# Another machine model orders the queues of a recurrence and expert-layer kernel on one core

## The chip, the cores and the metric

The kernel runs on one core of a Trainium2 chip. The metric is the device time of one execution in microseconds (us). TensorE (PE) multiplies, with its weight loads shown as PEld; VectorE (DVE), ScalarE (ACT) and GpSimd (POOL) work on elements; SyncE (SP) issues most of the DMAs. Each engine works through its own queue of instructions in order, and semaphores make an instruction wait for others.

## The reference

A gated linear recurrence over 768 tokens, for 4 sequences and 8 heads of width 48, and then a SiLU layer of width 2048 over all 3,072 tokens:

```
for t in range(S):
    state = alpha[:, :, t, :, None] * state + einsum('bhd,bhe->bhde', k[:, :, t], v[:, :, t])
    y[:, :, t] = einsum('bhd,bhde->bhe', q[:, :, t], state)
x = y.transpose(0, 2, 1, 3).reshape(B * S, H * D)
h = x @ w_in
out = (h * (1 / (1 + exp(-h)))) @ w_out
```

## The kernel before

The program has a quick path, `quotients` (L356), and a slow one, `general`, which is taken when a check of the inputs' sizes fails; with these inputs it is not taken. All below is `quotients`. The check's flag is loaded by each engine shortly before the end, with a hint for the branch.

**The work.** The 3,072 tokens are 24 chunks of 128, in six groups of four. A chunk goes through attention stages on several engines, and each group then through w_in, SiLU and w_out. From the second half of the second group on, products by w_in are made as 20 products of sums of blocks (`enter`, L943), and products by w_out as seven (`leave`, L1050).

The weights arrive as 64-bit floats and are converted on ScalarE (L637) and VectorE (L653 to L655) in the first stage.

**Attention, from the ninth chunk on.** `load` (L466) issues eight DMAs each for alpha, k and q of a chunk (L485) into the tiles at, kt and qt, of which there is one each. `beside` (L491) makes two ScalarE copies in each (L496). `turned` (L715) transposes a tile on VectorE (L716): at into al, kt and qt into the tile turn, of which there is one; behind it, `load` for the next chunk may begin. `products` scans (L742) and forms kp (L759, L761); `quotient` forms p by reciprocals (L772), a scan (L774) and a product (L780). `flip` (L782) transposes kp on VectorE into turn (L790) and stores it to the DRAM tile flips by a DMA of SyncE (L792); `land` (L794) brings it back as kn on GpSimd's queue. `scores` multiplies kp and p on TensorE, copies the result out of PSUM on ScalarE (L828, L831) and masks it on GpSimd; `values` multiplies with v and copies to xt (L873); `states` adds to the state on VectorE (L890).

**The layer.** `enter` has three PSUM banks (ps_m). A product goes into a bank, and ScalarE copies it out (L963) to g or part, or VectorE combines it there (L971). SiLU is L968. `side_by_side` adds halves (L1046), `leave` has two banks (ps_o) and subtracts parts of g (L1062); results are stored at L1074.

**The check of the inputs.** `audit` (L665) loads alpha and the weights anew and reduces them on VectorE (L706). Its last sixteen loads, those of w_out, land in at, kt and qt.

**What sets the order.** The code emits work in steps: `fill` deals out pieces of the layer between the attention stages of each step. The language then makes each engine's queue when the program is built: it runs the instructions through a model of the machine and issues what that model has ready, by priority. An instruction inside `tc.keep_in_program_order` stays behind what was emitted ahead of it on its engine. After `settle` (L1197), which opens the tiles of the later stages, all TensorE's instructions are held so (L381 to L392), and some of VectorE's: the sums of weights and tokens and the reductions of the check.

Of the kernel before, what the change touches and what calls it, by code (L numbers as in the profile page):

```python
# [1291 lines left out]
@with_exitstack  # L1292
def kernel(
    ctx: ExitStack,
    tc: tile.TileContext,
    q: bass.AP,
    k: bass.AP,
    v: bass.AP,
    alpha: bass.AP,
    moe_w_in: bass.AP,  # L1300
    moe_w_out: bass.AP,
    out: bass.AP,
):


    flag = ctx.enter_context(tc.tile_pool(name="flag", bufs=1))
    small = flag.tile([1, 1], I32, name="small")
    args = (q, k, v, alpha, moe_w_in, moe_w_out, out)
    within = quotients(tc, small, *args)
    with tc.If(within < 1, label="general"):  # L1310
        general(tc, *args)

# [29 lines left out]
```

## Time and profile before

| | |
|---|---|
| median of 3 runs | 557.59 us (557.36 to 560.03) |
| the profiled execution | 558.21 us |
| its span, first to last instruction | 556.5 us |
| granted clock of TensorE | 0.999 of full speed |
| TensorE busy | 539.6 us |
| VectorE busy | 440.8 us |
| ScalarE busy | 253.8 us |
| GpSimd busy | 106.8 us |
| mean DMA rate | 109 GB/s |

The span leaves out what comes ahead of the first and behind the last instruction. A line of the page's groups names line, engine, operation, what is written and read and its shape, the count, the busy time and the mean of one, and then the idle time of the engine just ahead of it with what ended it. A line of the waits names who waited for whom, the total in us, the times and the longest. A line of a time line has the start, the length, the engine (SPq is SyncE's sequencer, which issues DMAs), the operation and the count. A window's line has its ends, its length, and for PE, PEld, DVE, ACT and POOL the busy time and the instructions, and then TensorE's clock, the share of the DMA engines and GB/s. A line of DMA issues ends with the KB of each and the median us from issue to landing.

### The profile page before, as it was taken

The numbers are of one execution on the slowest core, as the hardware profiler recorded it, in microseconds if no ns is written. First come the engines' busy times: TensorE is split into PE (matmuls) and PEld (weight loads), VectorE is DVE, ScalarE is ACT, GpSimd is POOL, SyncE is SP. The second block draws the span as 40 slices with busy tenths as digits, with TensorE's granted clock in tenths as the row PEclk, the third lists the DMA queues.
The fourth block names the chain that finished last, engine by engine and source line by source line (L and its number), as shares of the span: only waits on it lengthen the run. The fifth ranks groups of instructions, "written<-read, shape, count | busy, mean of one in ns | idle before, by whom it ended". The sixth has DMA issues, their size and how long they took to land. (4 is left out here: it accounts for less than half of the span.)

```text
span 556.5 us, 13238 instructions
## 1 busy us (share of the span) xinstructions
PE 539.6 (97%) x5010; PEld 487.0 (88%) x5010; DVE 440.8 (79%) x826; ACT 253.8 (46%) x570; POOL 106.8 (19%) x194
## 2 busy tenths in 40 slices
PE   6999999999999899999999999999999999999995
PEld 4788887998898699899999898999998999999995
DVE  5897888987997899997997988897863896945431
ACT  2556653235564564573555465555453341423100
POOL 3110000222334213223214213212111000001000
PEclk9999999999999999999999999999999999999999
DMA  9988971134434434435646564446331135500000
GB/s 213 255 230 220 235 191 29 38 71 87 86 69 107 93 68 95 99 72 145 141 79 159 129 149 104 104 96 150 106 115 46 53 109 172 156 7 23 15 23 25
DMA packets 121496, 60.72 MB, mean 109 GB/s; under 512 B 108497, under 2 KB 110161, under 8 KB 121425
## 3 DMA queue, kind: packets, MB, share of 16 engines
q1 hardware_dynamic: 117968, 52.73, 40.7%
q0 software_dynamic: 3456, 7.08, 4.1%
q8 instruction: 40, 0.66, 0.5%
q14 instruction: 32, 0.25, 0.2%
HBM read 51.90 MB, written 7.86 MB: 107 GB/s over the span
## 5 line engine op out<-in xcount | busy, mean ns | idle before, releaser
L388 PE MATMUL ps_o<-w_out,g 128*128 128x192 f32 x768 | 134.0, 328 | 0.5 <-DVE o L1071 0.5
L388 PEld LDWEIGHTS ps_o<-w_out,g 128*128 128x128 f32 x768 | 125.6, 190 | 3.6 <-DVE o L1071 0.8
L388 PE MATMUL ps_o<-wt,g 128*128 128x192 f32 x576 | 99.8, 327 | 0.0
L388 PE MATMUL ps_m<-xt,w_in 128*128 128x256 f32 x396 | 94.8, 383 | 1.8 <-ACT xt L873 1.1
L388 PEld LDWEIGHTS ps_o<-wt,g 128*128 128x128 f32 x576 | 95.1, 190 | 1.6 <-issue 0.2
L388 PEld LDWEIGHTS ps_m<-xt,w_in 128*128 128x128 f32 x396 | 73.4, 190 | 13.3 <-ACT xt L873 1.6
L388 PE MATMUL ps_m<-xc,w_in 128*128 128x256 f32 x324 | 79.6, 382 | 1.1 <-DVE g L971 1.1
L388 PEld LDWEIGHTS ps_m<-xc,w_in 128*128 128x128 f32 x324 | 60.4, 190 | 9.1 <-DVE g L971 1.5
L1074 POOL DMA_DIRECT2D out_dram<-o x40 | 22.4, 559 | 202.6 <-DVE o L1071 102.6
L1062 DVE TENSOR_TENSOR g<-g 128x512 f32<-128x512 f32 x72 | 49.2, 698 | 9.1 <-PE ps_o L388 8.9
L388 PE MATMUL ps_m<-xc,wx 128*128 128x256 f32 x216 | 56.4, 383 | 0.0
L968 ACT ACTIVATE g<-g 128x1024 f32<-128x1024 f32 x36 | 37.1, 1055 | 40.8 <-DVE g L971 40.7
L963 ACT COPY g<-ps_m 128x512 f32<-128x512 f32 x72 | 40.8, 588 | 29.3 <-PE ps_m L388 28.8
L835 POOL TENSOR_SCALAR_AFFINE_SELECT g<-g 64x256 f32<-64x256 f32 x64 | 38.2, 596 | 60.2 <-ACT g L828 57.1
L971 DVE TENSOR_TENSOR g<-ps_m,g 128x512 f32<-128x512 f32 x63 | 41.9, 684 | 5.1 <-PE ps_m L388 4.2
L388 PEld LDWEIGHTS ps_m<-xc,wx 128*128 128x128 f32 x216 | 39.5, 190 | 4.7 <-ACT kt L496 0.2
L742 DVE TENSOR_TENSOR_SCAN u<-al,one 128x516 f32<-128x516 f32 x24 | 29.9, 1246 | 11.9 <-ACT al L739 11.7
L963 ACT COPY part<-ps_m 128x512 f32<-128x512 f32 x36 | 21.2, 589 | 37.5 <-DVE g L971 22.2
L800 POOL DMA_DIRECT2D kn<-flips x48 | 26.2, 553 | 49.2 <-PE ps_a L388 43.2
L774 DVE TENSOR_TENSOR_SCAN p<-al,inv 128x516 f32<-128x516 f32 x24 | 29.8, 1241 | 2.6 <-PE ps_a L388 2.1
L706 DVE TENSOR_REDUCE seen<-bits 128x1 f32<-128x512 int32 (+1 forms) x33 | 26.6, 825 | 5.7 <-DMA bits<-in_alpha_dram 2.9
L823 POOL TENSOR_SCALAR_AFFINE_SELECT g<-g 128x512 f32<-128x512 f32 x16 | 12.6, 808 | 85.8 <-ACT g L822 85.8
(133 smaller groups left out, 694.4 us busy)
## 6 DMA issues: line engine op xcount, KB each, us to landing
bits<-in_moe_w_in_dram SPq DMA_DIRECT2D x24, 512.0 KB, 4.3
bits<-in_moe_w_out_dram SPq DMA_DIRECT2D x16, 384.0 KB, 3.7
bits<-in_alpha_dram SPq DMA_DIRECT2D x9, 512.0 KB, 4.0
out_dram<-o POOLq DMA_DIRECT2D x40, 96.0 KB, 2.3
at<-in_alpha_dram SPq DMA_DIRECT2D x128, 24.0 KB, 2.3
kt<-in_k_dram SPq DMA_DIRECT2D x128, 24.0 KB, 2.1
qt<-in_q_dram SPq DMA_DIRECT2D x128, 24.0 KB, 2.0
flips<-turn SPq DMA_DIRECT2D x12, 256.0 KB, 4.3
```

Of the source, the lines that this page charges most:

```text
L388: in_order(nc.tensor.matmul(*args, **kw))
L706: dve.tensor_reduce(seen[kind][which][:, i : i + 1], x, axis=AX, op=op, apply_absolute_value=True))
L742: dve.tensor_tensor_scan(u[:, end - 1 :: -1], sg[:, end:0:-1], one[:, end:0:-1], 0.0, ALU.mult, ALU.add)
L774: dve.tensor_tensor_scan(p[:, 0:end], sg[:, 0:end], iv[:, 0:end], 0.0, ALU.mult, ALU.add)
L800: gps.dma_start(c["kn"][32 * i : 32 * i + 32], x[i])
L823: gps.affine_select(g[:, u], g[:, u], pattern=[[0, NP], [1, C]], compare_op=ALU.is_ge, fill=0.0, base=0, channel_multiplier=-1)
L835: gps.affine_select(x, x, pattern=[[0, NP], [1, CH]], compare_op=ALU.is_ge, fill=0.0, base=0, channel_multiplier=-1)
L963: act.copy(to, ps)
L968: act.activation(x, x, AF.Silu)
L971: dve.tensor_tensor(to, a, b, op)
L1062: dve.tensor_tensor(cells(grp, h, pair, *to), cells(grp, h, pair, *x), cells(grp, h, pair, *y), ALU.subtract)
L1074: (gps if grp < NG - 1 else nc.sync).dma_start(out[r : r + C, c * HO : (c + 1) * HO], o)
```

## The change

`quotients` is emitted inside a block whose queues are ordered by the language's other model of the machine. The instructions, tiles and pools stay as they are, the orders that the code pins too. The block is one of its own in the program, with a branch behind it to the place of the test of the flag.

```diff
     args = (q, k, v, alpha, moe_w_in, moe_w_out, out)
-    within = quotients(tc, small, *args)
+    with tc.block(name="quick", schedule_with_timeline_sim=True):
+        within = quotients(tc, small, *args)
     with tc.If(within < 1, label="general"):
         general(tc, *args)
```

## The prediction

> **What bounds the kernel now.** The first view is the page's busy times, the second the table of windows, the third TensorE's own waits.
>
> ```profile
> span 556.5 us, 13238 instructions
> PE 539.6 (97%) x5010; PEld 487.0 (88%) x5010; DVE 440.8 (79%) x826; ACT 253.8 (46%) x570; POOL 106.8 (19%) x194
> ```
>
> ```profile
> 109.00:200.00 91.00, 87.42 (x992) 78.28 (x991) 78.07 (x156) 48.88 (x126) 30.77 (x50) 1.00 0.42 83
> 200.00:250.00 50.00, 49.87 (x475) 45.63 (x474) 49.34 (x97) 28.52 (x67) 11.62 (x21) 1.00 0.40 82
> 250.00:300.00 50.00, 50.00 (x579) 45.59 (x578) 44.33 (x79) 25.32 (x61) 12.88 (x24) 1.00 0.55 131
> ```
>
> ```profile
> PE ps_a L388 <- DVE p L780: 1.6, 2, 0.9
> PE ps_m L388 <- DVE g L971: 1.4, 2, 1.1
> PE ps_m L388 <- ACT part L963: 0.6, 1, 0.6
> PE ps_o L388 <- DVE o L1071: 0.5, 1, 0.5
> PE ps_m L388 <- ACT xt L873: 0.3, 1, 0.3
> ```
>
> TensorE is the bound: from 109 us to the end it stands idle 4.4 us (the sum of the last view, taken over that window), at a granted clock of 1.00 (the column behind POOL). So an order can win little there. What it can lose shows in the second row: between 200 and 250 us VectorE is busy 49.34 of 50 us. A wait put into its queue there has no idle time to go into.
>
> The other views are those of the loop that brings in alpha, k and q: the page's DMA issues, and the time lines of SyncE, ScalarE and VectorE around 240 us.
>
> ```profile
> at<-in_alpha_dram SPq DMA_DIRECT2D x128, 24.0 KB, 2.3
> flips<-turn SPq DMA_DIRECT2D x12, 256.0 KB, 4.3
> ```
>
> ```profile
> 239.93 3.63 SPq L485 DMA_DIRECT2D kt<-in_k_dram  x8
> 243.66 3.71 SPq L485 DMA_DIRECT2D qt<-in_q_dram  x8
> ```
>
> ```profile
> 238.86 1.07 ACT L963 COPY g<-ps_m 128x512 f32<-128x512 f32 x2
> 239.82 0.60 ACT L963 COPY part<-ps_m 128x512 f32<-128x512 f32 x1
> 240.71 0.94 ACT L496 COPY at<-at 32x256 f32<-32x256 f32 x2 [0.28 <-DMA at<-in_alpha_dram]
> ```
>
> ```profile
> 235.42 0.72 DVE L890 TENSOR_TENSOR st<-ps_a,st 48x192 f32<-48x192 f32 x2
> ```
>
> **The change part by part.** It keeps every instruction (2,569 matmuls, 637 DMAs in both programs) and moves them in the queues: 335 of TensorE's matmuls, 445 of VectorE's 826 instructions, 354 of ScalarE's 569, 263 of SyncE's 551 issues.
>
> *TensorE.* All its moves lie ahead of 109 us; behind that its order is the same, matmul for matmul. Ahead of it, transposes and small matmuls stand between other products than before, and the number of changes from one kind to the next goes from 262 to 265. I cost this at 0. From 24 us on TensorE is hardly idle in that stretch (48.92 of 50 us busy between 50 and 100), so a gain has some 3 us to go into; a few more waits on the conversions of the weights would cost as much. Bounds: -3 and +3.
>
> *The end.* Each engine gets one more branch. VectorE's compare-and-branch starts at 550.80 and its next record stands at 551.40: 0.6 us. The last store, issued at 551.16, lands at 553.75 and covers it. Cost 0; without that cover 0.6.
>
> *The loop of the loads.* One buffer each holds alpha, k and q of a chunk (at, kt, qt). VectorE transposes it (L716), which frees it; SyncE then issues eight loads; ScalarE makes two copies (L496) behind their landing. The rows give the length of a loop from the end of the transpose: seven issues at 0.475 us (3.71 over eight, with the gap) are 3.3, the eighth lands 2.3 later, 5.6 in all, and the two copies take 0.8: 6.4 us. ScalarE works in order, so a copy that stands too early holds up the copies out of PSUM behind it (L963, 0.59 each), which free the banks for which TensorE's next product waits.
>
> I took both orders and put TensorE's times of the profile beside them. For each of these pairs of copies that carries a wait on VectorE, the room is a difference: TensorE's time for which the first instruction behind the copy in ScalarE's queue waits, less TensorE's time for which the last instruction up to the transpose waits in VectorE's queue, less VectorE's work from there through the transpose. Between 200 and 430 us, in the order before, the rooms are 8.8, 11.1, 9.8, 18.5, 12.7, 5.6 and 9.7: one below 6.4. In the order after they are for at 6.2, 4.4, 6.2, 4.4, 6.2, 4.4, 6.5, 7.6; for qt 5.3, 5.9, 5.1, 4.8, 4.4; for kt 5.4, 10.7, 10.9, 6.9, 10.2, 4.3. Thirteen of nineteen are short, by 16.2 us in all, and that with a VectorE that is never late.
>
> It is late. Take the chunk of 232 to 253 us. Its states matmuls (ps_a<-vn,kn) end on TensorE at 232.49 (231.97 plus 0.52); the additions that wait for them alone start at 235.42 in the row above: a lag of 2.9. After the change VectorE has there the two additions and at once the next transpose of at (1.1 of work): done at 232.5 + 2.9 + 1.1 = 236.5, landed at 242.1. ScalarE's queue is: a copy of PSUM, one copy of at, a second of PSUM, the other of at, the third of PSUM. So the second ends at 242.1 + 0.4 + 0.6 = 243.1 where TensorE starts on that bank at 242.21, and the third at 244.1 where it wants 243.07. Before, they ended at 239.93 and 240.42. That is 1.0 us late. A shorter room of the neighbouring chunks works alike; I take 1.0 for each of the ten chunks of 21 us between 211 and 430 us: **10**. From below it is 0: with no lag, a room of 4.4 is 2.0 short, and the bank has 2.3 to spare (239.93 to 242.21). From above all of ScalarE's lateness reaches TensorE: 6.4 + 2.9 - 4.4 = 4.9 a chunk, 49.
>
> *The wait that VectorE gets.* The tile turn has one buffer. The transpose of kp into it (L790) is stored by the DMA to flips, and the next transpose of kt writes it again, so it must wait until that DMA has landed, 4.3 us after its issue. VectorE's work between the two is, for the seven such chunks from 212 us on, 9.3, 7.8, 6.0, 9.8, 3.9, 7.2 and 5.2 us before, and 3.2, 3.6, 1.9, 2.7, 1.9, 2.9 and 3.9 after. Short of 4.3 by 1.1, 0.7, 2.4, 1.6, 2.4, 1.4 and 0.4: **10.0**. Behind that transpose stand the combinations of the products (L971) and the halves' sums (L1062); TensorE waits for both. SyncE's pending loads ahead of the store would add to it; VectorE's 5.7 idle us of the third row of windows would take from it. I take it whole; bounds 0 and 20 (3.7 more, eight loads ahead of the store, in about half of them).
>
> *Between 109 and 200 us.* Chunks are 14 to 19 us here, SyncE issues almost without a break, and the rooms are 7.7 and more. One place is worse: the pair of at that ran at 174.90 now stands between copies that ran at 165.27 and 165.75. Its loads were issued from 168.21; SyncE's one idle gap of the forty us before is 2.5 us, so the earliest landing is 168.2 - 2.5 + 5.6 = 171.3, and the bank behind it is wanted at 167.20. That is 4.1, and I take **4**; bounds 0 and 8 (a second such place).
>
> *The sum.* The profiled execution took 558.21 us for its span of 556.5; the median of the runs is 557.59, 0.6 less. 558.2 + 0 + 10 + 10 + 4 = **582**.
>
> [...]
>
> **The rivals.**
> - *The loop in full* (0.11): every lateness of ScalarE reaches TensorE, 4.9 in each of ten chunks, and 4: 558.2 + 49 + 4 = 611. For it: TensorE without slack, and both delays in one ring. Against it: a late TensorE gives VectorE its lag back.
> - *Absorbed* (0.07): VectorE, which waits less for TensorE in the new order, loses its lag of 2.9; the 2.0 that are missing fit into the bank's 2.3: 558. Against it: 49.34 of 50.
> - *Faster* (0.08): the attention steps that stand earlier take away TensorE's waits on p, g and part. All of them gone is 4.4: 553.8. It decides in the loop: if the loads land within 4.4 us of the transpose, copies included, no room is short. Against it: one issue alone is 0.475, and eight are needed.
> - *No change*, because the order does not change: excluded for VectorE and ScalarE by the moves above, true for TensorE from 109 us on.
>
> **How the numbers follow.** The forecast has 0.74, so the likeliest time is 582. Its low end: 4 for the early place with nothing else passed on, 562. Its high end: twice each of the two tens, and 8, is 606. That holds 0.74 at most, so the range goes on to the loop in full: 562 to 612. Outside are the rivals at 0.08 and 0.07, both below. Half a per cent, 2.8 us, is what a measurement of this kernel can tell from none: faster 0.08, same 0.07, slower 0.74 + 0.11 = 0.85.
>
> **What would show it.** ScalarE's waits on the DMAs of at, kt and qt (34 us over the whole run before: 15.8, 9.3, 9.1) should more than double; VectorE should wait for flips at the transpose of kt, which it does not before; TensorE's waits on L963 and L971 should go from 2 us to some 20, spread over 160 to 430 us, with the stretch behind 430 us as long as before. If ScalarE waits for the loads but TensorE's waits stay small, the absorption is right. If ScalarE does not wait more, the loop of 6.4 is wrong.

## The result, and the profile after

The changed kernel takes 596.38 us (median of 4 runs, 594.82 to 597.96), the kernel before beside it 557.48: a ratio of 1.0688, 95% interval 1.064 to 1.0736. The profiled execution took 597.96 us. Its page begins:

```profile
span 596.1 us, 13255 instructions
PE 554.6 (93%) x5010; PEld 496.2 (83%) x5010; DVE 439.0 (74%) x826; ACT 253.8 (43%) x570; POOL 105.2 (18%) x194
```

The span is 39.6 us longer. VectorE and ScalarE have the same work as before, and TensorE has 15.0 us more busy time for the same matmuls, for which the prediction has no term. The table of windows shows where TensorE stands (first figure behind the length: its busy time; behind POOL: its granted clock):

```profile
109.00:160.00 51.00, 47.47 (x516) 42.71 (x516) 39.48 (x84) 21.15 (x59) 13.02 (x23) 0.97 0.35 69
160.00:215.00 55.00, 46.70 (x539) 39.99 (x538) 44.43 (x84) 29.37 (x74) 14.54 (x28) 0.97 0.43 88
270.00:325.00 55.00, 50.38 (x539) 45.02 (x538) 42.40 (x77) 23.89 (x56) 13.33 (x24) 0.97 0.43 102
440.00:596.00 156.00, 149.91 (x998) 141.08 (x990) 92.45 (x176) 44.76 (x87) 9.93 (x20) 1.00 0.22 67
```

The last 156 us are as before (150.17 busy then, 149.91 now). The loss lies ahead of them, and part of it is clock: 0.97 in three of the rows, where before all had 1.00.

A matmul can be followed from one trace to the other, since TensorE's order is the same from 109 us on. The delay of its start, after less before, is by before's clock 3.4 us at 109 us, 3.7 at 126, 8.4 at 139, 12.3 at 170, 17.8 at 200, 20.9 at 274, 29.7 at 320, 37.6 at 369, 39.7 at 394 and 39.7 at 550: about 3 in the start, 14 between 109 and 200, 22 between 200 and 394, nothing behind. Two lists of waits say on whom (total us, times, longest). TensorE's:

```profile
PE ps_a L388 <- ACT xt L873: 7.1, 4, 2.8
PE ps_m L388 <- DVE xc L594: 6.1, 3, 3.6
PE ps_m L388 <- ACT xt L873: 4.4, 2, 3.5
...
PE ps_m L388 <- ACT g L963: 3.2, 3, 1.5
PE ps_m L388 <- DVE g L971: 3.1, 4, 1.2
PE ps_o L388 <- ACT g L968: 2.7, 2, 2.2
PE ps_m L388 <- ACT part L963: 2.5, 3, 1.1
```

and ScalarE's for the loads (two lines of the list):

```profile
ACT kt L496 <- DMA kt<-in_k_dram: 47.9, 16, 6.1
...
ACT qt L496 <- DMA qt<-in_q_dram: 22.2, 13, 3.8
```

With 15.3 and 9.2 for at, ScalarE stands 94.6 us before those copies; it was 34.2. Behind 109 us TensorE waits 19.0 us for ScalarE (0.9 before) and, with 0.5 for o, 9.7 for VectorE (3.5 before). (Of the 4.4 us of the third line, one wait of 0.9 lies ahead of 109 us.)

One wait read through all queues, the longest on xt (time lines of ScalarE, SyncE and TensorE):

```profile
125.76 0.83 ACT L496 COPY kt<-kt 32x256 f32<-32x256 f32 x2 [3.82 <-DMA kt<-in_k_dram]
129.32 0.89 ACT L496 COPY qt<-qt 32x256 f32<-32x256 f32 x2 [2.73 <-DMA qt<-in_q_dram]
133.10 0.40 ACT L496 COPY at<-at 32x256 f32<-32x256 f32 x1 [2.89 <-DMA at<-in_alpha_dram]
133.53 0.48 ACT L873 COPY xt<-ps_a 128x384 f32<-128x384 f32 x1
```

```profile
119.76 4.67 SPq L485 DMA_DIRECT2D kt<-in_k_dram  x7
124.52 3.73 SPq L485 DMA_DIRECT2D qt<-in_q_dram  x8
128.36 3.70 SPq L485 DMA_DIRECT2D at<-in_alpha_dram  x8
```

```profile
134.06 4.33 PE L388 MATMUL ps_m<-xt,w_in 128*128 128x256 f32 x12 [3.53 <-ACT xt L873]
```

ScalarE's queue has the copies of kt, qt and at one behind the other, and the copy to xt behind them. SyncE issues one tile behind the other, 3.7 us each and 5.3 for kt (the first of its eight loads lies ahead of this view), so each copy waits its turn, and TensorE stands 3.53 us for a copy of 0.48. The tile at had been free since 120.95 (its transpose ran from 120.24 for 0.71); its loads were issued from 128.36, behind those of kt and qt.

Windows of the same place:

```profile
132.00:134.00 2.00, 0.00 (x0) 0.00 (x0) 1.97 (x6) 0.88 (x2) 0.70 (x3) 0.92 0.45 102
134.00:136.00 2.00, 1.94 (x5) 1.58 (x6) 1.96 (x6) 0.41 (x2) 0.00 (x0) 0.50 0.30 48
136.00:138.00 2.00, 2.00 (x8) 1.70 (x7) 2.00 (x5) 0.00 (x0) 0.00 (x0) 0.73 0.19 34
138.00:140.00 2.00, 2.00 (x38) 1.52 (x37) 1.97 (x6) 1.59 (x4) 0.00 (x0) 1.00 0.36 53
```

When TensorE goes on, its clock is at half for some 3.4 us. Such a phase lies at the end of four of the waits (those ending at 134, 170, 298 and 405 us, the last phase 6.8 us long). Over windows of 1 us, busy share times the missing clock comes to 7.5 us.

The account of the 39.7 us of delay: the start 3.4 and, behind it, more waits for ScalarE 18.1, more waits for VectorE 6.2, half speed 7.5. That is 35.2. The other 4.5 are busy time of TensorE: behind 109 us it is busy 12.1 us longer (449.3 for 437.2), of which half speed explains 7.5; the rest stays open.

### The profile page after: what moved, and what is told of

The parts are those of the page before. It is cut to its first block, busy times and chain, and to the rows that moved or that the text cites. A ratio compares the mean times of both kernels' runs of the same rounds, so it can differ in the third digit from the quotient of the medians.

```text
span 596.1 us, 13255 instructions
## 1 busy us (share of the span) xinstructions
PE 554.6 (93%) x5010; PEld 496.2 (83%) x5010; DVE 439.0 (74%) x826; ACT 253.8 (43%) x570; POOL 105.2 (18%) x194
## 5 line engine op out<-in xcount | busy, mean ns | idle before, releaser
L388 PE MATMUL ps_o<-w_out,g 128*128 128x192 f32 x768 | 136.3, 331 | 3.2 <-ACT g L968 2.7
L388 PEld LDWEIGHTS ps_o<-w_out,g 128*128 128x128 f32 x768 | 127.6, 192 | 6.8 <-ACT g L968 3.1
L388 PE MATMUL ps_m<-xc,w_in 128*128 128x256 f32 x324 | 83.0, 393 | 7.4 <-ACT g L963 3.2
L388 PEld LDWEIGHTS ps_m<-xt,w_in 128*128 128x128 f32 x396 | 74.8, 193 | 16.8 <-ACT xt L873 4.7
L388 PE MATMUL ps_m<-xc,wx 128*128 128x256 f32 x216 | 58.6, 395 | 6.1 <-DVE xc L594 6.1
L963 ACT COPY g<-ps_m 128x512 f32<-128x512 f32 x72 | 41.8, 588 | 28.8 <-PE ps_m L388 27.9
L968 ACT ACTIVATE g<-g 128x1024 f32<-128x1024 f32 x36 | 37.1, 1054 | 36.7 <-DVE g L971 36.4
L971 DVE TENSOR_TENSOR g<-ps_m,g 128x512 f32<-128x512 f32 x63 | 42.3, 682 | 4.6 <-PE ps_m L388 4.0
L388 PEld LDWEIGHTS ps_a<-p,kp 48*64 48x64 f32 (+1 forms) x640 | 24.9, 151 | 16.4 <-ACT xt L873 8.0
L388 PE MATMUL ps_a<-p,kp 48*64 48x64 f32 (+2 forms) x640 | 30.5, 264 | 8.2 <-ACT xt L873 7.1
L496 ACT COPY kt<-kt 32x256 f32<-32x256 f32 x32 | 12.9, 402 | 48.5 <-DMA kt<-in_k_dram 47.9
L800 POOL DMA_DIRECT2D kn<-flips x48 | 26.2, 553 | 39.6 <-PE ps_a L388 34.9
L774 DVE TENSOR_TENSOR_SCAN p<-al,inv 128x516 f32<-128x516 f32 x24 | 29.7, 1236 | 4.2 <-PE ps_a L388 3.8
```

Of the source, the lines that this page charges most:

```text
L388: in_order(nc.tensor.matmul(*args, **kw))
L496: act.copy(ctxs[n][name][64 * u + 32 : 64 * u + 64, :, :, 0 : D - 32], ctxs[n][name][r, :, :, 32:D])
L774: dve.tensor_tensor_scan(p[:, 0:end], sg[:, 0:end], iv[:, 0:end], 0.0, ALU.mult, ALU.add)
L800: gps.dma_start(c["kn"][32 * i : 32 * i + 32], x[i])
L963: act.copy(to, ps)
L968: act.activation(x, x, AF.Silu)
```

## The experiments

Theories at the outset. **L**: ScalarE's copies stand too soon behind the loads, and the copies out of PSUM wait behind them. **V**: VectorE's new order holds TensorE up (sums, flips, turns). **S**: SyncE issues the loads in a bad order. After the first runs **A**: loads and VectorE's sums of x, each a trouble of its own; and **C**: a long wait costs clock as well.

Most kernels hold a queue in a given order. They are the changed kernel with the list of one engine's instructions, by number, and edges that only order the issue; what is not listed is ordered by the other model anew, so a free queue is not quite that of the changed kernel.

```diff
+    at = {i.name: i for i in nc.cur_bb.bb.instructions}
+    for queue in QUEUES:
+        for x, y in zip(queue, queue[1:]):
+            tc.add_manual_dep(at[f"I-{y}"], f"I-{x}", mybir.DependencyInfo(
+                mybir.DependencyClass.NoSync, mybir.DependencyReason.DATA), reason="queue")
     return within
```

Lines of these kernels' profiles are shifted by their lists; the text gives the line of the code above.

### The block without the other model

```diff
-    with tc.block(name="quick", schedule_with_timeline_sim=True):
+    with tc.block(name="quick"):
```

> The block stays, the other machine model goes: the queues of PE, DVE, ACT and SP are those of before, instruction for instruction, with one more branch on each engine. All theories: the time of before, 557.5, within 1.7 us. If the block itself (its branches) cost anything, the time would be above 560 and part of the 39 us would have nothing to do with the order.

Measured: 559.47 us, ratio 1.0012 (0.9989 to 1.0035). The block and its branches cost nothing that can be measured; the order is the cause.

### One engine's queue as before

> The changed kernel, but ScalarE's 569 instructions are held in the order that they had before; PE, DVE and SP are ordered by the other model around them. Counted as in the prediction, no room behind the loads of at, kt and qt is then short of 6.4 us (smallest 10.2, against 13 short rooms after the change). VectorE's work between the turn of kp and the next turn into the same tile is short of 4.3 us by some 5 us in all. Theory L (ScalarE's copies stand too soon behind the loads, and the copies out of PSUM wait behind them): only the flips and the start are left, 557.5 + 5 + 4 = 566. Theory V (VectorE's new order holds TensorE up: sums, flips, turns): little comes back, 585 to 595. Theory S (SyncE issues the loads in a bad order): 580 to 595, since SP's order is nearer to after than to before.

> The changed kernel, but VectorE's 826 instructions are held in the order that they had before; PE, ACT and SP are ordered by the other model. Rooms short of 6.4 us: 4 of 15 between 109 and 200 us, 10 of 18 behind, 15.0 us in all (after: 16.2). No wait for flips beyond before's. Theory L: most of the loss stays, 557.5 + 39 less the flips (7) = 589, 582 to 594. Theory V: at most 566. Theory S: 580 to 595.

> The changed kernel, but SyncE's 551 issues are held in the order that they had before; PE, DVE and ACT are ordered by the other model. Rooms short of 6.4 us: 6 of 11 between 200 and 430 us, by 7.3 us in all (after: 13 by 16.2). Theory L: somewhat under half of what is lost behind 200 us stays, and the places around 130 to 190 us stay as ACT has them: 572 to 584. Theory V: 588 to 597. Theory S: at most 566.

Measured: ScalarE's queue as before 584.12 (1.0449, 1.0419 to 1.048); VectorE's 585.12 (1.0464, 1.043 to 1.0499); SyncE's 593.51 (1.064, 1.0594 to 1.0685). Of the 38.9 us that the change costs, 13.7, 12.7 and 4.3 came back (each against the 558.95 of the kernel before, run beside them). None of the three theories holds alone: L had 566 for the first, V and S at most 566 for the second and the third.

With ScalarE's queue as before, its waits for at, kt and qt are down to 14.8 us, and yet the delay is 26 us. TensorE's waits there (L641 is L594, L1018 is L971):

```profile
PE ps_m L435 <- DVE xc L641: 6.6, 3, 3.1
...
PE ps_m L435 <- DVE g L1018: 3.7, 2, 3.1
```

They are VectorE's: the sums of x and the combinations. (The line left out, 4.2 us for the first load, stands before the change too, with 4.3.) With VectorE's queue as before, ScalarE's list is (L559 is L496):

```profile
ACT kt L559 <- DMA kt<-in_k_dram: 50.2, 18, 5.9
ACT at L559 <- DMA at<-in_alpha_dram: 33.0, 16, 4.3
```

With qt that is 102.7 us, more than in the changed kernel. So each queue has a trouble of its own.

VectorE's is read best in the changed kernel's time line (lines between left out):

```profile
394.74 0.42 DVE L590 TENSOR_TENSOR xc<-xt 128x256 f32<-128x256 f32 x1
...
396.28 0.41 DVE L590 TENSOR_TENSOR xc<-xt,xc 128x256 f32<-128x256 f32 x1
...
397.43 1.26 DVE L706 TENSOR_REDUCE seen<-bits 128x1 f32<-128x512 int32 x2
...
400.58 1.18 DVE L742 TENSOR_TENSOR_SCAN u<-al,one 128x516 f32<-128x516 f32 x1
...
402.88 1.28 DVE L706 TENSOR_REDUCE seen<-bits 128x1 f32<-128x512 int32 x2
404.07 0.42 DVE L594 TENSOR_TENSOR xc<-xc,xt 128x256 f32<-128x256 f32 x1
```

Each group has eleven sums of x (L590 to L595), and the products wait for them one after another. Here the reductions of the check and a scan stand among them: from the first of these lines to the L594 on which TensorE waited 3.61 us it is 9.3 us, and was 5.2 before. From the third sum to the last, starts compared, groups two to four take 12.8, 9.7 and 12.8 us, and took 6.0, 6.9 and 6.5.

### Both queues as before

> The changed kernel with the orders of before on both ScalarE and VectorE; PE (ahead of 109 us) and SP are ordered by the other model. With one of the two put back 26 us stayed with ScalarE's, 28 with VectorE's: neither alone is the carrier. Theory A (each of the two queues has a trouble of its own: ScalarE's copies too soon behind the loads, VectorE's sums of x and turns too late; with both put back both are gone): 557.5 and the start's 3 to 4, 561, 558 to 566. Theory S (the order of SyncE's issues holds up whichever queue there is): 572 or more, since SP's order is the other model's in all three.

Measured: 568.7 us, ratio 1.0196 (1.0148 to 1.0243). 26.9 us came back, nearly the sum of 13.7 and 12.7, as theory A has it; but 12 are left where it had at most 8.5, so the two queues are not all. The delay is 3.9 at 109 us and 6.9 at 126 (a wait of 2.43 for VectorE, which has stood 2.39 at the turn of at), and 3.3 more come near 316 us: TensorE waits 1.88 us for L971 and runs at half speed behind it, and VectorE stood 2.72 us before that for a load of the check, which SyncE had issued among those of at. Behind 109 us every engine but SyncE works here in the order of before, so these are the order of SyncE's issues: a third, small part.

### Only the start, only the rest

> All five queues hold the order of before for the instructions traced ahead of the first load of at; behind them the other model orders VectorE, ScalarE and SP. The delay of the changed kernel against before stood at 3.6 us at 115 us and at 39.7 at the end. Theory A, if the start's 3.6 simply add: 596.4 - 3.6 = 593, 588 to 597. If the lateness of the start is what upsets the rest (every later wait follows from it): 575 or less.

> The reverse: the instructions traced ahead of the first load of at are ordered as in the changed kernel, those behind as before. If the start's 3.6 simply add: 557.5 + 3.6 = 561, 559 to 564. If the start is worth nothing by itself: 557.5 within 1.7. If its lateness upsets the rest: over 570.

Measured: 596.14 us (1.0711, 1.0683 to 1.074) with the old start and the new rest; 562.42 (1.0093, 1.0057 to 1.013) with the new start and the old rest. By itself the new start costs 5.7 us, of which 4.1 stand at 109 us in the profile. Taken away from the changed kernel it gives nothing back. That the rest has enough waits into which 4 us disappear is the likely reason, but not shown: the other model ordered that rest anew, and up to 226 us ScalarE and VectorE have some instructions in other places than in the changed kernel. Either way the parts are no simple sum.

### Half of the loads

```diff
-            for g in range(NP):
+            for g in range(NP // 2):
                 for u in range(2):
                     nc.sync.dma_start(c[name][64 * u : 64 * u + 32, g],
```

with all five queues held as in the changed kernel.

> The changed kernel with the same order on all engines, but of the eight loads of each alpha, k and q tile from the ninth chunk on only four are issued (it leaves out the loads of four of the eight heads there; their places keep the filling). The loop gets shorter by four issues of 0.475: 6.4 to 4.5 us, and SP's queue is relieved by 192 issues, 91 us of its time. Rooms short of it: five of 4.3 to 4.4, by 0.7 us in all, instead of thirteen by 16.2. Theory A: what goes by the loads returns, the sums of x and the flips stay: 570 to 582. Theory V (the order of VectorE alone, ScalarE's waits being covered): 590 to 597.

Measured: 570.29 us, ratio 1.0235 (1.0217 to 1.0252). 25 of the 39 us are gone with no instruction of TensorE, VectorE or ScalarE in another place. A load lands no sooner than with all of them (median for kt 1.84 us behind its issue, 1.89 in the changed kernel), so what is saved is issues, and the time for which other DMAs stand behind them in SyncE's queue. ScalarE's waits for the loads fell to 17.0 us. What is left of TensorE's waits behind 100 us (L930 is L594; 7.7 us, three waits):

```profile
PE ps_m L724 <- DVE xc L930: 7.7, 3, 3.1
```

### The sums of x moved

VectorE's list is that of the changed kernel with 24 instructions moved; the other four queues are held too.

> The changed kernel with the same order on all engines, except that on VectorE the last nine of the eleven sums of x (L590 to L595, into xc) of the second, third and fourth group stand with one other instruction between two of them, as they did before, instead of up to six. By the durations of before, the work from the third sum to the last falls from 12.5, 9.6 and 12.7 us to 7.3, 7.2 and 7.3 (before: 5.9, 6.7, 6.3). Theory A (the sums are VectorE's own trouble): TensorE's 6.1 us of waits on the sums (L594) go and with them the half speed behind the wait of 3.61 (3.4 us); some of it is taken up by ScalarE's waits for the loads, which stay: 587, 583 to 593. If the sums are late only because the loads are: 594 to 598.

> Both: half of the loads of alpha, k and q from the ninth chunk on (the other half is left out), and the sums moved; the rest as in the changed kernel. With half of the loads 570.3 us, and TensorE's only long waits behind 100 us are three on the sums, 2.1, 2.5 and 3.1 us, each with 3.3 us at half speed behind it (1.7 lost). Theory A, that loads, sums and start are all of it: 570.3 - 7.7 - 5.0 = 557.6, and not under 557.5 + 3.6 - 1 for the start, so 558 to 563. If a third cause of some size is hidden under the two: over 565.

Measured: sums alone 598.05 us (1.0734, 1.0709 to 1.0759), nothing back where theory A had 583 to 593; with half of the loads 564.92 (1.0112, 1.0071 to 1.0153), 5.4 less than half of the loads alone (6.0 when each is set against the kernel before run beside it) and above the 558 to 563 expected. In the first, the waits on L594 are gone from the list, and the one of 3.61 us with them; ScalarE's copies out of PSUM hold TensorE instead:

```profile
PE ps_m L738 <- ACT part L1313: 7.9, 5, 3.0
PE ps_m L738 <- ACT xt L1223: 4.7, 2, 3.8
```

(L1313 is L963; it was 2.5 for part.) With half of the loads TensorE waited even longer for the sums than in the changed kernel (7.7 us for 6.1), so they are not late because of the loads: they are a trouble of their own, but one that runs beside the loads, and it shows only when those are short. In the second, one wait of 3.02 us on L963 is left, with 6.8 us at half speed behind it, some 6 in all; ScalarE stood 5.04 us for qt before it.

### The copies in program order

```diff
-                act.copy(ctxs[n][name][64 * u + 32 : 64 * u + 64, :, :, 0 : D - 32],
-                         ctxs[n][name][r, :, :, 32:D])
+                tc.keep_in_program_order(
+                    act.copy(ctxs[n][name][64 * u + 32 : 64 * u + 64, :, :, 0 : D - 32],
+                             ctxs[n][name][r, :, :, 32:D]))
```

> The changed kernel with one wish more to the scheduler: the copies of at, kt and qt (L496) stay in program order on ScalarE; everything else is ordered by the other model. No room is then short of 6.4 us in either stretch; VectorE's work from the third sum of x to the last is 6.9, 10.7, 8.3 and 7.8 us in the first four groups (before: 7.5, 5.9, 6.7, 6.3; changed: 8.7, 12.5, 9.6, 12.7). Theory A: the start's 3.6, one late group of sums (about 3 us with its half speed) and small change: 566, 561 to 574. If the loss comes back at other instructions as it did with ScalarE's whole queue put back: 575 to 588.

Measured: 572.89 us, ratio 1.0291 (1.0261 to 1.0321): with this wish 23 of the 39 us are gone. Not the copies alone have moved: the other model orders the rest anew, and 323 of ScalarE's 570 places and 413 of VectorE's 826 hold another instruction than in the changed kernel. The delay is 4.2 at 139 us, 6.7 at 180, 14.3 at 200 and 14.0 at the end. The 7 us of one place are a wait on VectorE, which waits for the tile turn (SyncE, VectorE and TensorE; L793 is L792, L717 is L716):

```profile
177.85 3.74 SPq L485 DMA_DIRECT2D kt<-in_k_dram  x7
181.69 3.70 SPq L485 DMA_DIRECT2D qt<-in_q_dram  x8
185.48 0.38 SPq L793 DMA_DIRECT2D flips<-turn  x1
```

```profile
187.87 0.71 DVE L717 STREAM_TRANSPOSE turn<-kt 128x512 f32<-128x512 f32 x1 [6.19 <-DMA vn<-in_v_dram]
```

```profile
193.50 2.08 PE L388 MATMUL ps_m<-xt,wx 128*128 128x256 f32 x4 [5.25 <-DVE g L972]
```

The transpose of kp had ended at 179.74, but its store to flips stood in SyncE's queue until 185.48, behind eleven of these loads that were still to be issued. (The page names vn, the DMA whose end came nearest; vn is no input of that transpose. The copies of kt had ended at 183.84.) This is the wait for flips of the prediction, and here it reaches TensorE nearly whole.

### A wait of known length, put into the kernel before

```diff
         add(b, True)
+        for _ in range(HOLD.pop(0)):
+            act.copy(scratch, scratch)
         copy(b, s[2])
```

with HOLD = 5, 6, 8, 9, 11, 13, 15, 17, 20, scratch a tile of 128x128, and all queues of the kernel before held.

> The kernel before, its order held on all engines, with 5, 6, 8, 9, 11, 13, 15, 17 and 20 small copies (128x128, some 0.27 us each) on ScalarE ahead of one copy out of PSUM in each of nine products of four blocks. TensorE must wait for that bank: by 1.3 to 5.4 us less the bank's slack of about 1, some 19 us in all. Theory C (a wait of more than about 2 us makes the clock fall to half for 3.3 or 6.7 us behind it, 1.7 or 3.4 lost): the delay at the end is larger than the sum of the waits by 8 to 17, 557 + 19 + 12 = 588. If a wait costs itself alone: the delay is the sum of the waits, about 576, and matmuls behind each wait keep their 0.216 us.

Measured: 570.32 us, ratio 1.0227 (1.0202 to 1.0252): 12.95 us. A small copy took 0.298 us, and the waits were shorter than I had reckoned, 9.5 us in six, the bank having more slack:

```profile
PE ps_m L746 <- ACT g L1324: 9.5, 6, 2.4
```

Two of them, of 2.41 and 2.43 us, have half speed behind them; those of 1.10, 1.44 and 1.76 have none. Windows around the one of 1.76 (first two rows) and the one of 2.41:

```profile
370.00:372.00 2.00, 0.24 (x2) 0.16 (x2) 0.64 (x1) 1.89 (x6) 0.00 (x0) 1.00 0.57 186
372.00:374.00 2.00, 2.00 (x11) 1.79 (x11) 1.69 (x3) 1.38 (x4) 0.00 (x0) 1.00 0.29 51
...
414.00:416.00 2.00, 0.00 (x0) 0.00 (x0) 0.00 (x0) 1.87 (x7) 0.00 (x0) 1.00 0.00 0
416.00:418.00 2.00, 1.88 (x5) 1.59 (x6) 1.41 (x3) 1.41 (x5) 0.00 (x0) 0.62 0.00 0
418.00:420.00 2.00, 2.00 (x7) 1.64 (x7) 1.08 (x2) 0.88 (x2) 0.00 (x0) 0.52 0.48 121
420.00:422.00 2.00, 2.00 (x14) 2.00 (x13) 1.39 (x2) 0.20 (x1) 0.00 (x0) 1.00 0.39 150
```

The delay steps from 2.92 to 5.60 over the wait of 2.41, and on to 7.39 while the clock is low: 1.8 more. At 2.43 it is 9.00, 11.69 and 13.39: 1.7 more. 9.5 + 1.8 + 1.7 is 13.0, close to the 12.95 measured. So a wait can cost clock as well, as theory C has it; that a wait costs itself alone is refuted. Two parts of C failed: the clock cost 3.5 us and not 8 to 17, and a limit of about 2 us is not what decides, since in the kernel with both queues as before a wait of 1.88 us has half speed behind it and one of 2.43 has none.

## Why the prediction was right, and where its sizes were wrong

The sign, the kind and the range were right: slower, through ScalarE's and VectorE's waits in the loop of the loads, 596 in 562 to 612. The forecast of 582 was 14 us short. Step by step:

- *The end, 0.* Right: the delay is the same 39.7 us at 394 and 550 us, and the block alone costs nothing.
- *TensorE's order ahead of 109 us, 0 (-3 to +3).* 3.4 us at 109 us in the profile, 5.7 by itself in time: beyond the bound. That stretch has nearly as much idle time as before (7.1 us, 6.6 then); 3.0 us of the loss are busy time. It is not the order of ScalarE or VectorE, since with both as before 3.9 are still there at 109 us. It is mostly clock. The profile's clock records begin with full speed at 19.04 us before and at 24.44 after (its clock column shows 1.00 ahead of them, too, and the granted clocks of 0.999 and 0.984 over the span leave that time out); ahead of them the same transposes take half as long again. TensorE's groups from 19.5 to 24 us, before and after (count, busy time, mean ns):

```profile
L392 PE MATMUL ps_a<-ident,kp 128*128 128x128 f32 x4 | 0.7, 286 | 0.0
```

```profile
L392 PE MATMUL ps_a<-ident,kp 128*128 128x128 f32 x4 | 1.1, 431 | 0.0
```

They follow one another every 0.11 and 0.21 us. TensorE is busy throughout these 5.4 us; at half speed that is 2.7 of the 3.4 us. With the start of before, full speed came at 17 to 20 us in every kernel here; with the new start at 24 to 27 in seven of ten, but at 10.0 and 11.3 in the two with half of the loads, where 2.4 and 2.9 us of delay are there all the same, and at 7.6 with ScalarE's queue as before, which fell back to half from 14.4 to 24.7. Why the new order keeps TensorE at half speed longer stays open.
- *The loop of the loads, 10, and between 109 and 200 us, 4.* The mechanism was right: half the loads, or their copies in another place, give back 25 and 23 us (both help SyncE's other DMAs too, so some of it is the flips'). The size was wrong by nearly half, and mostly ahead of 200 us: the delay grew there by 14.4 where I had 4, bound 8. My rooms there were 7.7 us and more against a loop of 6.4. But 6.4 is the loop of one tile with SyncE free. Its landing of 2.3 us was not too short: the loads landed a median of 2.3, 2.1 and 2.0 us behind their issue (at, kt, qt) before and 1.9 after. Where the copies of three tiles stand together, SyncE issues 24 loads in one go, and the tile at waited from 120.95 to 128.36 for its turn. I had written that SyncE issues almost without a break there, and took no time for it. Behind 200 us the delay grew by 21.9, near the 10 + 10 of the forecast; that confirms neither term, since the sums, which had no term, are in it and the flips hardly.
- *The wait for flips, 10.* VectorE's own wait came near in the sum, and not chunk by chunk: ahead of the turn of kt in the seven chunks from 212 us on it stood 11.8 us (0, 1.2, 4.3, 2.6, 0, 2.8, 0.8), where kt had landed long before. Two stores landed in 2.0 and 2.9 us and held up nothing; the other five stood in SyncE's queue for 1.0 to 3.0 us first, for which the prediction had taken nothing in its 10. The prediction's reading that VectorE does not wait for flips before the change is wrong. There, too, it stood 4.1, 2.1, 0.8 and 1.9 us at the turn of kt until the store to flips had landed (at 139.63, 170.13, 294.57 and 333.88 us); the profile puts these down to another DMA that ended close by:

```profile
140.00 0.71 DVE L716 STREAM_TRANSPOSE turn<-kt 128x512 f32<-128x512 f32 x1 [4.06 <-DMA at<-in_alpha_dram]
...
334.00 0.71 DVE L716 STREAM_TRANSPOSE turn<-kt 128x512 f32<-128x512 f32 x1 [1.91 <-DMA at<-in_alpha_dram]
```

So the wait grew, over the whole run from 8.8 us to 24.1, and was not new. What failed is "I take it whole": TensorE waited directly behind the seven only 0.74 and 0.95 us. The same wait with SyncE's loads ahead of the store, for which I had 3.7 as an upper bound, reached TensorE with 5.25 us in the kernel with the pinned copies.
- *Not priced: the sums of x.* I named the combinations and the halves' sums as what stands behind VectorE's transpose, and did not look at where the eleven sums went. They are 6.1 us of TensorE's waits; the runs give 5.4 for them once the loads are short and nothing before, so they are no term to be added but a second bound beside the first.
- *Not priced: the clock.* 7.5 us behind 109 us, beside the 2.7 in the start. Before, TensorE has no wait over 1.2 us behind 109 us and the clock is 1.00 there.

Of the signs named, ScalarE's waits more than doubled (34.2 to 94.6), VectorE waits longer at the turn of kt, and behind 394 us nothing changed. TensorE's waits on L963 and L971 went to 8.8 us and not to 20; with xt (L873) and SiLU (L968), which stand in the same queue, ScalarE alone has 19.0. The rival "absorbed" is refuted, and "the loop in full" (611) was as far off as the forecast. So the total came out in the range partly by luck: some 8 us too many on the flips stood against loads, clock, sums and start that were too small or missing.

## What to carry to other kernels

Where one queue issues the loads of several one-buffer tiles, the time from a tile's release to its landing was here the issues queued ahead plus its own, not its own alone (at was free at 120.95 us, its loads were issued from 128.36 and its copies began at 133.10); ask where each load and each store stands in that queue before judging an order of the engines that wait for it. An instruction that waits for a load should be held where its engine has nothing urgent behind it: with such a wish on 96 copies, and the rest ordered anew around them, 23 of 39 us were gone here. And parts of a loss that lay beside each other did not add: the sums gave nothing alone (598.05 us for 596.38) and 5.4 us with half of the loads, the old start nothing alone (596.14), though the new one costs 5.7 by itself.

## What the hardware showed that I had not expected

A wait of TensorE can cost more than itself: those of 2.41 and 2.43 us in the kernel with the small copies cost 1.8 and 1.7 us more. Behind 100 us, each of the fourteen waits of 3.0 us or more in these traces had half the granted clock at its end or within 1.5 us behind it, for 3.4 or 6.8 us in all, so up to 1.7 or 3.4 us lost; of the shorter ones some had (1.88, 2.19, 2.41, 2.43), some had not (2.43 with both queues as before, 2.59 with the pinned copies, 2.81 at 186 us of the changed kernel). So equal waits fare differently, and their length alone does not decide; what does was not shown. At the start full speed came only at 19.0 us before the change, though TensorE was, by the profile, busy 4.6 us or more of each 5 from 5 us on; behind the later waits it came back after 3.4 or 6.8 us. Why the start takes longer stays open too.

The twelve stores to flips of either trace landed in one of two times, with nothing between: 2.0 to 2.9 us or 4.2 to 4.7 us behind their issue. Before, five of the twelve are short and seven long; after, eight and four, so the median falls from 4.3 to 2.8 us. What decides between the two was not looked into.

```profile
flips<-turn SPq DMA_DIRECT2D x12, 256.0 KB, 2.8
```
